# One more folding of the odd rows of a Fourier transform, and product tiles of more than 64 rows

## The chip, the cores and the metric

One core of one Trainium2 chip. The time is that of the device for one execution, in microseconds (us), on the slowest core; here there is only the one. A figure for a kernel is the median of its timed runs. PE is TensorE (PEld its weight loads, which put the stationary operand of a product in place), DVE is VectorE, ACT is ScalarE, POOL is GpSimd. PSUM and SBUF are the two memories of the core that the kernel works in: its products are written to PSUM, which it uses in parts called banks; most else lies in SBUF. A "product" below is one matmul of the source; in float32 it is two PE instructions.

## The reference, cut to what matters

```python
def _attn_ref(x):                       # x: 8 x 3008 x 256
    X = np.fft.fft(x, axis=1)
    X = np.fft.fft(X, axis=2)
    return X.real.astype(np.float32)

def _moe_ref(x, w_in, w_out):           # 24064 x 256, 256 x 2048, 2048 x 256
    h = x @ w_in
    r = np.maximum(h, 0.0)
    g = r * r
    return (g @ w_out).astype(np.float32)
```

Eight sequences of 3008 rows. The transform along the rows is a product with cosine and sine tables. Row n and row 3008 - n have equal cosines and opposite sines, so rows are added and subtracted ("folded") before the product, which halves its length; the same is done again for other symmetries of the table.

## The kernel before: the parts that matter here

Each sequence takes 48 steps: 6 blocks of 251 (or 250) columns by 8 chunks of the hidden layer. A step makes four products `ph` (into the hidden layer), evaluates relu squared, and does seven products `mA` to `mD` of the step two before (out of the hidden layer). While sequence b is in its steps, the transform of sequence b + 1 is done on the side, cut into small pieces that `between()` slips in after each half of a step, at a steady pace.

```python
def class_tiles(S):                    # rows of the folded transform, in classes
    half = S // 8 + 1
    tiles = []
    for c, order in enumerate((range(0, half, 4), range(2, half, 4), range(1, half, 2), range(half, S // 4 + 1))):
        for r in range(0, len(order), P):                       # P = 128
            tiles.append((c, order[r], order.step, len(order[r:r + P])))
    return tiles                       # 95 | 94 | 128, 60 | 128, 128, 120 rows

    def fold(b, t): ...                # DVE: makes wP, wQ of tile t of sequence b

    def dft_ops(b):
        def group(kp, which):          # kp: even or odd k; which: P (cosine) or Q (sine)
            def product(ps, c):
                for t in ts:           # the tiles of class c
                    nc.tensor.matmul(ps, w, tab[0:rows, kp, PLACE[t]:PLACE[t] + NC[kp][c]],
                                     start=t == ts[0], stop=t == ts[-1])
            def even_n():              # classes 0, 1, 2: 95, 94, 128 and 60 rows
                ...
            def odd_n():               # class 3: 128, 128 and 120 rows, 376 or 377 columns
                st["odd"] = psd.tile([P, 512], F32, name="pd", tag="d")[0:n, 0:n0]
                product(st["odd"], 3)
            # join_4, join_2, join_1: DVE adds and subtracts the parts
    ...
    def between():                     # called after each half of a step
        nonlocal spent
        if i < 2 * NJ:
            return
        spent -= pace
        while side and spent <= 0:
            t, f = side.pop(0)
            f()
            spent += t
```

"E" is one special column of the transform, done once for all later sequences while sequence 0 is in its steps.

## Time and profile before

| | before |
|---|---|
| median of 3 runs | 1990.51 us (1989.71 to 1991.41) |
| span of the profiled run | 1991.9 us |
| PE busy | 1957.8 us, 98% |
| DVE, ACT, POOL busy | 70%, 45%, 58% |
| one sequence in its steady state | 237.8 us, PE busy in all of it |

The first rows say that PE sets the time; the last, that it does so without a pause. A saving must therefore be PE time, and a new cost on another engine matters only where PE comes to wait for it. The lines themselves are in the prediction.

### The profile page before, as it was taken

Reading aid. Unit: us, or ns where it says so; the run is one execution under the profiler, and the core shown is the slowest. Engines: PE = TensorE matmul, PEld = TensorE weight load, DVE = VectorE, ACT = ScalarE, POOL = GpSimd, SP = SyncE. Lnnn points to the kernel's source line nnn. Section 1 sums busy time; section 2 is a strip of 40 time slices with the busy share of each in tenths; the row PEclk is TensorE's granted clock in tenths of the full one; section 3 lists DMA queues with packets and bytes.
Section 4 is the critical chain, followed back from the end, with each engine's and each line's share of the span. In section 5 each row is a group of like instructions: output and inputs, shape, how many; then the busy total and the mean of one; then the engine's idle time right before and its main releaser. Section 6 shows DMA issues by size and latency. Waiting matters only on the chain.

```text
span 1991.9 us, 27283 instructions
## 1 busy us (share of the span) xinstructions
PE 1957.8 (98%) x9104; PEld 1701.1 (85%) x9104; DVE 1391.3 (70%) x3492; ACT 896.2 (45%) x973; POOL 1158.8 (58%) x1695
## 2 busy tenths in 40 slices
PE   6999999999999999999999999999999999999998
PEld 3788888888888888888888888888888888888887
DVE  7889867776578765787558875677756876555554
ACT  1654444444444444444344443444444444445443
POOL 0037646666566655666557665666656675566664
PEclk8999999999999999999999999999999999999999
DMA  6331101110011111111011110121002100100100
GB/s 190 110 39 47 38 11 37 47 27 22 18 46 32 40 19 27 27 41 39 11 32 32 39 30 11 32 51 29 22 11 52 32 11 16 32 11 11 22 11 21
DMA packets 144687, 68.49 MB, mean 34 GB/s; under 512 B 128440, under 2 KB 135547, under 8 KB 144546
## 3 DMA queue, kind: packets, MB, share of 16 engines
q1 hardware_dynamic: 143470, 66.24, 14.1%
q8 instruction: 71, 1.16, 0.2%
q14 instruction: 70, 0.57, 0.1%
q10 hardware_dynamic: 1076, 0.52, 0.1%
HBM read 42.03 MB, written 24.68 MB: 33 GB/s over the span
## 4 chain that ended last, share of the span: by engine, by line
PE 94%; DVE 2%; DMA 1%; ACT 1%; SPq 0%; issue 0%; DVEq 0%; ACTq 0%
PE ph L412 16%; PE ph L413 16%; PE mA L465 16%; PE mC L465 16%; PE mB L465 16%; PE mD L465 8%; PE pd L349 5%; DMA xt<-in_x_dram 1%; DMA raw<-in_moe_w_in_dram 1%; DVE he L415 0%; DVE g L418 0%; ACT g L427 0%; ACT g L428 0%; SPq L163 0%; DVE g L417 0%
## 5 line engine op out<-in xcount | busy, mean ns | idle before, releaser
L427 ACT ACTIVATE g<-g 128x1004 f32<-128x1004 f32 (+1 forms) x384 | 399.6, 1041 | 894.3 <-DVE g L418 511.1
L415 DVE SCALAR_TENSOR_TENSOR he<-Et,gE,ph 128x251 f32<-128x251 f32 (+1 forms) x768 | 361.8, 471 | 476.6 <-PE ph L413 475.1
L435 POOL TENSOR_TENSOR s<-g 128x251 f32<-128x251 f32 (+1 forms) x376 | 248.9, 662 | 739.3 <-ACT g L428 668.1
L412 PE MATMUL ph<-Pt,G 128*128 128x251 f32 (+1 forms) x1536 | 453.4, 376 | 4.5 <-ACT G L237 3.4
L413 PE MATMUL ph<-Qt,G 127*128 127x251 f32 (+1 forms) x1536 | 451.3, 374 | 0.2 <-DVE Qt L362 0.2
L428 ACT ACTIVATE g<-g 128x1004 f32<-128x1004 f32 (+1 forms) x384 | 399.3, 1040 | 12.1
L465 PE MATMUL mC<-s,wsum 128*128 128x251 f32 (+1 forms) x1504 | 381.3, 374 | 0.0
L465 PE MATMUL mA<-g,wout 128*128 128x251 f32 (+1 forms) x1504 | 381.0, 375 | 0.0
L417 DVE TENSOR_TENSOR g<-he,ph 128x251 f32<-128x251 f32 (+1 forms) x768 | 320.6, 417 | 55.6 <-POOL s L437 0.5
L412 PEld LDWEIGHTS ph<-Pt,G 128*128 128x128 f32 x1536 | 287.2, 189 | 48.7 <-ACT G L237 4.0
L413 PEld LDWEIGHTS ph<-Qt,G 127*128 127x128 f32 x1536 | 291.1, 190 | 36.4 <-DVE Qt L362 0.6
L465 PEld LDWEIGHTS mA<-g,wout 128*128 128x128 f32 x1504 | 282.5, 189 | 41.7 <-issue 2.9
L465 PEld LDWEIGHTS mC<-s,wsum 128*128 128x128 f32 x1504 | 285.5, 190 | 34.5
L418 DVE TENSOR_TENSOR g<-he,ph 128x251 f32<-128x251 f32 (+1 forms) x768 | 314.2, 409 | 0.0
L436 POOL TENSOR_TENSOR s<-s,g 128x251 f32<-128x251 f32 (+1 forms) x376 | 282.0, 750 | 29.4
L437 POOL TENSOR_TENSOR s<-g 128x251 f32<-128x251 f32 (+1 forms) x376 | 291.4, 775 | 0.0
L438 POOL TENSOR_TENSOR s<-g,s 128x251 f32<-128x251 f32 (+1 forms) x376 | 246.0, 654 | 0.0
L465 PE MATMUL mB<-g,wsum 128*128 128x251 f32 (+1 forms) x752 | 220.5, 374 | 0.0
L465 PE MATMUL mD<-s,wout 128*128 128x251 f32 (+1 forms) x752 | 220.3, 374 | 0.0
L465 PE MATMUL mB<-s,wout 128*128 128x251 f32 (+1 forms) x752 | 219.9, 374 | 0.0
L465 PEld LDWEIGHTS mB<-g,wsum 128*128 128x128 f32 x752 | 142.6, 190 | 17.4
L465 PEld LDWEIGHTS mD<-s,wout 128*128 128x128 f32 x752 | 141.9, 189 | 17.7
(85 smaller groups left out, 1264.3 us busy)
## 6 DMA issues: line engine op xcount, KB each, us to landing
out_dram<-os SPq DMA_DIRECT2D x376, 56.0 KB
xt<-in_x_dram SPq DMA_DIRECT2D x24, 512.0 KB
xt<-in_x_dram SPq DMA_DIRECT2D x16, 384.0 KB
Et<-e_dram SPq DMA_DIRECT2D x7, 752.5 KB
out_dram<-os SPq DMA_DIRECT2D x288, 6.8 KB
raw<-in_moe_w_in_dram SPq DMA_DIRECT2D x16, 256.0 KB
raw<-in_moe_w_out_dram SPq DMA_DIRECT2D x16, 256.0 KB
xt<-in_x_dram SPq DMA_DIRECT2D x8, 480.0 KB
```

The lines of the kernel that those rows point to most:

```text
L412: nc.tensor.matmul(hP, G1[:, fs], pt[:, ks], start=True, stop=True)
L413: nc.tensor.matmul(hQ, G2[:, fs], qt[:, ks], start=True, stop=True)
L415: nc.vector.scalar_tensor_tensor(out=t, in0=et[:, ks], scalar=gE[:, fc:fc + 1], in1=hP, op0=ALU.mult, op1=ALU.add)
L417: tt(out=g[:, h, 0, 0:n], in0=t, in1=hQ, op=ALU.add)
L418: tt(out=g[:, h, 1, 0:n][:, ::-1], in0=t, in1=hQ, op=ALU.subtract)
L427: act(v, v, AF.Relu)
L428: act(v, v, AF.Square)
L435: gt(out=s1, in0=g21, in1=g22, op=ALU.add)
L436: gt(out=s2, in0=s1, in1=g11, op=ALU.subtract)
L437: gt(out=s3, in0=g11, in1=g21, op=ALU.subtract)
L438: gt(out=s4, in0=g12, in1=s2, op=ALU.subtract)
L465: nc.tensor.matmul(acc[nm][:, i, 0:n], w, v[:, 0:n], start=j == 0 and i == 0, stop=j == NJ - 1, skip_group_check=True)
```

## The change

The odd n of the later sequences are folded once more: row n is combined with the row mirrored within the odd set, and the cosine and sine parts of k even and odd part ways. The product is then over two tiles in place of three, for each half of the columns by itself. It needs, per sequence, a reversal of rows (a shuffle on DVE and loads in pieces of 32 rows), additions, and multiplications by a cosine and a sine per row. 188 mirrored rows are 128 + 60; the 60 are padded with zeros to 128. The tables of the odd class are sorted into even and odd columns once, after the pass for E, which still uses them unsorted. And the class of 188 rows is cut into 96 and 92, not 128 and 60. The side work of sequence 0 starts a block earlier, at half pace.

```diff
+        size = -(-len(order) // -(-len(order) // P) // R) * R          # 96
-        for r in range(0, len(order), P):
-            tiles.append((c, order[r], order.step, len(order[r:r + P])))
+        for r in range(0, len(order), size):
+            tiles.append((c, order[r], order.step, len(order[r:r + size])))
 ...
+        def f_turn():
+            w = w_of(t)
+            if i == 0:
+                st["v"], st["w"] = w_of(ODD0), w
+                nc.vector.stream_shuffle(w, w, REVERSE)
+            else:
+                st["v"], st["w"] = w, w_of(NT)
+                nc.vector.stream_shuffle(st["w"][0:H // 2], w[H // 2:P], REVERSE)
+                nc.gpsimd.memset(st["w"][H // 2:P], 0.0)
+            spare("f0", "f0")
+            nc.scalar.copy(st["f0"][rows], st["v"][rows, 0])
+        def spare(nm, tag):
+            st[nm] = fp.tile([P, D], F32, name=nm, tag=tag, bufs=1)
+            return st[nm]
+        def sine(to, src, signs):
+            for part, a in zip(PART, signs):
+                nc.scalar.mul(to[rows, part], src[rows, 1, part], turn[rows, 1 + a, i:i + 1])
+        def f_even():
+            v, w, a = st["v"][rows, 0], st["w"][rows, 0], st["f0"][rows]
+            tt(out=v, in0=a, in1=w, op=ALU.add)
+            tt(out=w, in0=a, in1=w, op=ALU.subtract)
+            sine(spare("f1", "f1"), st["w"], (0, 1))
+            sine(spare("f2", "f0"), st["v"], (1, 0))
+        def f_odd(): ...                                   # two scalar_tensor_tensor on DVE
 ...
             def odd_n():
+                for part in range(2):
+                    if kp:   ...  to = ps[:, part * nq:part * nq + nq]
+                    else:    ...  to = ps[:, part:n0:2]            # every second column of PSUM
+                    for i, pair in enumerate(((ODD0, ODD0 + 1), (ODD0 + 2, NT))):
+                        nc.tensor.matmul(to, folded[b, pair[other]][:, kp, PART[which]][:, 0:n],
+                                         columns(tab, ODD0 + i, o), start=i == 0, stop=i == 1)
 ...
-        if i < 2 * NJ:
+        if i < NJ:
             return
-        spent -= pace
+        spent -= pace / 2 if i < 2 * NJ else pace
```

(Cut: the loads, the sorting of the tables on ACT, the joins of the new parts for odd k, the weights of the pieces, and the order of the side work of sequence 0, in which the pass for E now comes before the groups of sequence 1.)

More of the change, by code (lines that the diff above doesn't have):

```diff
@@ L112 @@
     fp = ctx.enter_context(tc.tile_pool(name="fp", bufs=2))
-    wp = ctx.enter_context(tc.tile_pool(name="wp", bufs=NT))
+    wp = ctx.enter_context(tc.tile_pool(name="wp", bufs=NT + 1))
     pq = ctx.enter_context(tc.tile_pool(name="pq", bufs=2))
@@ L129 @@
     xt = {}
-    def load_x(b, t):
-        _, r0, step, rows = TILES[t]
+    ODD0 = NT - 3
+    HALF = S // 16
+    REST = HALF - P
+    ODD = [[(0, 0, P)],
+           [(p, 2 * HALF - p - R, R) for p in range(0, P, R)],
+           [(0, P, H // 2)] + [(H // 2 + p, 2 * HALF - P - p - R, R) for p in range(0, H // 2, R)]]
+    assert H == P and REST <= H // 2 and TILES[ODD0][0] == 3 and TILES[ODD0 + 1][1] == TILES[ODD0][1] + P
+    def load_x(b, t):
+        c, r0, step, rows = TILES[t]
+        if b and c == 3:
+            xt[b, t] = xp.tile([P, 4, D], F32, name="xt", tag="x")
+            for p, first, count in ODD[t - ODD0]:
+                nc.sync.dma_start(out=xt[b, t][p:p + count], in_=x[b, S // 8 + 1 + first:S // 8 + 1 + first + count])
+            return
         while rows % 15 and rows % 16 and r0 + step * rows < NROW:
@@ L263, with make_turn, part_table, columns @@
     PQE = {}
+    PART = (slice(0, H + 1), slice(H + 1, D))
+    REVERSE = list(range(R - 1, -1, -1))
+    turn = const.tile([P, 3, 2], F32, name="turn")
+    def make_turn():
+        for i in range(2):
+            for a, tab in enumerate((cosT, sinT, sinT)):
+                nc.scalar.mul(turn[:, a, i:i + 1], tab[:, 1, PLACE[ODD0 + i]:PLACE[ODD0 + i] + 1], -1.0 if a == 2 else 1.0)
+    rows_used = const.tile([P, 1], F32, name="rows_used")
+    nc.vector.memset(rows_used, 0.0)
+    nc.vector.memset(rows_used[0:REST], 1.0)
+    def part_table(tab, i):
+        nk, at = NC[0][3], PLACE[ODD0 + i]
+        v = tab[:, 0, at:at + nk]
+        a = op.tile([P, nk], F32, name="tp", tag="os")
+        nc.scalar.mul(a, v, rows_used if i else 1.0)
+        nc.scalar.copy(v[:, 0:(nk + 1) // 2], a[:, 0::2])
+        nc.scalar.copy(v[:, (nk + 1) // 2:], a[:, 1::2])
+    def columns(tab, t, part):
+        nk, at = NC[0][3], PLACE[t]
+        nq = (nk + 1) // 2
+        return tab[:, 0, at + part * nq:at + (nk if part else nq)]
     NE = B - 1
@@ L266 @@
     e_dram = dp.tile([NE, NKT], F32, name="e_dram")
-    e_rows = const.tile([NE, NKT], F32, name="e_rows")
     def load_column(t):
@@ L285, in fold @@
     def fold(b, t):
-        r = slice(0, TILES[t][3])
+        odd = b > 0 and t >= ODD0
+        r = slice(0, P if odd else TILES[t][3])
         st = {}
@@ L312, in f_dc, with w_of @@
             tt(out=new(fp, "dc", [P, 2, H - 1])[r], in0=d[r, :, 1:H], in1=d[r, :, D - 1:H:-1], op=ALU.subtract)
+        def w_of(t):
+            if (b, t) not in folded:
+                folded[b, t] = wp.tile([P, 2, D], F32, name="w", tag="w")
+            return folded[b, t]
         def f_p():
-            sc, wP = st["sc"], new(wp, "wP", [P, 2, H + 1])
+            sc, w = st["sc"], w_of(t)
             for kp in range(2):
-                tt(out=wP[r, kp], in0=sc[r, 0], in1=sc[r, 1], op=ALU.subtract if kp else ALU.add)
@@ L318, in f_p @@
-            folded[b, t, 0] = wP
+                tt(out=w[r, kp, PART[0]], in0=sc[r, 0], in1=sc[r, 1], op=ALU.subtract if kp else ALU.add)
         def f_q():
-            dc, wQ = st["dc"], new(wp, "wQ", [P, 2, H - 1])
+            dc, w = st["dc"], w_of(t)
             for kp in range(2):
-                tt(out=wQ[r, kp], in0=dc[r, 0], in1=dc[r, 1], op=ALU.add if kp else ALU.subtract)
-            folded[b, t, 1] = wQ
-        return [(0.7, f_s), (0.7, f_d), (0.5, f_sc), (0.4, f_dc), (0.6, f_p), (0.6, f_q)]
+                tt(out=w[r, kp, PART[1]], in0=dc[r, 0], in1=dc[r, 1], op=ALU.add if kp else ALU.subtract)
@@ new lines, in fold @@
+        ops = [(0.9, f_s), (0.9, f_d), (1.2, f_sc), (0.6, f_dc), (0.9, f_p), (0.7, f_q)]
+        if not odd or t == ODD0:
+            return ops
+        i = t - ODD0 - 1
+        rows = slice(0, TILES[ODD0 + i][3] if i == 0 else REST)
+        def f_turn():
[9 more added lines that the diff above has]
+            nc.scalar.copy(st["f0"][rows], st["v"][rows, 0])
@@ L328, in dft_ops, with f_odd @@
+        def f_odd():
+            for nm, u in (("f1", "v"), ("f2", "w")):
+                u = st[u][rows, 1]
+                nc.vector.scalar_tensor_tensor(out=u, in0=u, scalar=turn[rows, 0, i:i + 1], in1=st[nm][rows],
+                                               op0=ALU.mult, op1=ALU.add)
+        return ops + [(0.8, f_turn), (1.2, f_even), (1.4, f_odd)]
     def dft_ops(b):
@@ L345, in product @@
                     rows = TILES[t][3]
-                    w = we[t] if b is None else folded[b, t, which % 2]
-                    w = w[0:rows, kp]
+                    w = (we[t] if b is None else folded[b, t][:, :, PART[which % 2]])[0:rows, kp]
                     w = w[:, H:H + 1].to_broadcast([rows, n]) if which == 2 and b is not None else w[:, 0:n]
@@ L378, in odd_n, with join_odd @@
             def odd_n():
-                st["odd"] = psd.tile([P, 512], F32, name="pd", tag="d")[0:n, 0:n0]
-                product(st["odd"], 3)
+                ps = psd.tile([P, 512], F32, name="pd", tag="d")[0:n]
+                st["odd"] = ps[:, 0:n0]
+                if not b:
+                    return product(ps[:, 0:n0], 3)
+                nq = (n0 + 2) // 2 if kp else (n0 + 1) // 2
+                for part in range(2):
+                    if kp:
+                        tab, o = (cosT, sinT)[part], 0
+                        to = ps[:, part * nq:part * nq + nq]
+                        other = part != which
+                    else:
+                        tab, o = (cosT, sinT)[which], part
+                        to = ps[:, part:n0:2]
+                        other = part != which
+                    for i, pair in enumerate(((ODD0, ODD0 + 1), (ODD0 + 2, NT))):
+                        nc.tensor.matmul(to, folded[b, pair[other]][:, kp, PART[which]][:, 0:n],
+                                         columns(tab, ODD0 + i, o), start=i == 0, stop=i == 1)
+                if kp:
+                    st["cos"] = hp.tile([P, nq], F32, name="oc", tag="oc", bufs=1)[0:n]
+                    nc.scalar.copy(st["cos"], ps[:, 0:nq])
+                    st["sin"] = ps[:, nq:2 * nq]
+            def join_odd():
+                a, ps = st["cos"], st["sin"]
+                nq = a.shape[-1]
+                st["odd"] = o = hp.tile([P, NC[1][3]], F32, name="do", tag="do", bufs=1)[0:n, 0:n0]
+                tt(out=o[:, 0::2], in0=a[:, 0:nq - 1], in1=ps[:, 0:nq - 1], op=ALU.add)
+                if which == 1:
+                    tt(out=o[:, 1::2], in0=ps[:, 1:nq], in1=a[:, 1:nq], op=ALU.subtract)
+                else:
+                    tt(out=o[:, 1::2], in0=a[:, 1:nq], in1=ps[:, 1:nq], op=ALU.subtract)
             def join_1():
-                dst = e_rows if b is None else PQE[b][which]
+                dst = PQE[1][2][0:n] if b is None else PQE[b][which]
                 nh = S // 8
@@ L386, in join_1 @@
                      st["odd"])
-            return [(0.5, even_n), (0.5, join_4), (0.7, join_2), (0.0, odd_n), (1.2, join_1)]
+            ops = [(0.1, even_n), (0.5, join_4), (0.7, join_2), (0.1, odd_n), (1.0, join_1)]
+            if b and kp:
+                ops.insert(4, (0.7, join_odd))
+            return ops
         ops = [] if b is None else [(0.0, start)]
@@ L394, in dft_ops @@
         if b is None:
-            ops.append((0.0, lambda: nc.sync.dma_start(out=e_dram[:, :], in_=e_rows)))
+            ops.append((0.0, lambda: nc.sync.dma_start(out=e_dram[:, :], in_=PQE[1][2][0:NE])))
         return ops
@@ L533, in ahead @@
     def ahead(b):
-        ops = [piece for t in range(NT) for piece in fold(b, t)] + dft_ops(b)
-        if b == 1:
-            ops += [(0.6, lambda t=t: fold_column(t)) for t in range(NT)] + dft_ops(None)
-        return ops + [(0.0, lambda: load_e(b))] if b else ops
+        folds = [piece for t in range(NT) for piece in fold(b, t)]
+        if b > 1:
+            return folds + dft_ops(b) + [(0.0, lambda: load_e(b))]
+        start, *groups = dft_ops(1)
+        tables = [(0.3, lambda tab=tab, i=i: part_table(tab, i)) for i in range(2) for tab in (cosT, sinT)]
+        return (folds + [start] + [(0.6, lambda t=t: fold_column(t)) for t in range(NT)] + dft_ops(None) + tables
+                + groups + [(0.0, lambda: load_e(1))])
     weights = [lambda j=j: load_win(j) for j in range(2)]
@@ L630 @@
                 load_column(i - NJ)
+            if i == NJ:
+                make_turn()
             if i % per == 0:
@@ L633 @@
                 side = ahead(b + 1) if b + 1 < B else []
-                spent, pace = 0.0, sum(t for t, _ in side) / (2 * (per - (0 if i else 2 * NJ)) - 6)
+                spent, pace = 0.0, sum(t for t, _ in side) / (2 * per - 6 - (0 if i else 3 * NJ))
             g = front(b, k0, n, j, between)
```

## The prediction

> **What bounds the kernel now.** I read the page's busy shares first, then equal windows over the run, then the chain of work that ended last inside one period, then the weight loads around one small product.
>
> ```profile
> PE 1957.8 (98%) x9104; PEld 1701.1 (85%) x9104; DVE 1391.3 (70%) x3492; ACT 896.2 (45%) x973; POOL 1158.8 (58%) x1695
> ```
>
> ```profile
> 467.20:704.90 237.70, 237.70 (x1114) 208.23 (x1113) 167.24 (x418) 107.27 (x113) 148.90 (x216) 1.00 0.13 30
> 704.90:942.70 237.80, 237.80 (x1115) 208.35 (x1114) 167.42 (x418) 107.36 (x113) 148.88 (x216) 1.00 0.13 30
> ```
>
> The window columns are the stretch, its length, then busy us (and instructions) of PE, PEld, DVE, ACT and POOL, clock, DMA share, GB/s. One sequence takes 237.8 us (the same spot in the chain recurs at 467.16, 704.93, 942.70), and PE is busy in all of it at full clock: no wait, no transfer and no other engine sets the time there. The others have room (DVE 167.4 of 237.8, ACT 107.4, POOL 148.9). So what PE no longer does in a period comes off the end, as long as the others still keep up. The chain of waits within a period says what a sequence's transform costs PE:
>
> ```profile
> 963.50 0.42 PE ph L413 x2
> 963.92 1.28 PE pd L349 x8
> 965.20 0.62 PE ph L412 x2
> 965.83 0.42 PE ph L413 x2
> ...
> 974.33 0.43 PE ph L413 x2
> 974.75 1.90 PE pd L349 x6
> 976.65 0.42 PE ph L412 x2
> ```
>
> Columns: start, us on the chain, what. Each product in the source is two PE instructions. The eight are the even-n half of a group (tiles of 95, 94, 128 and 60 rows), the six its odd-n half (three tiles of 376 or 377 columns). Two things to see: the six take 1.90 us, 317 ns each for 376 columns; and the pair after the eight takes 0.62 us where every other such pair takes 0.42, so an even half really costs 1.28 + 0.20 = 1.48 us. The weight loads show why:
>
> ```profile
> 963.76 0.64 PEld L349 LDWEIGHTS pd<-cosT,wP 95*128 95x128 f32 x5
> 964.62 0.29 PEld L349 LDWEIGHTS pd<-cosT,wP 60*128 60x128 f32 x2 [0.22 <-issue]
> 965.13 0.19 PEld L412 LDWEIGHTS ph<-Pt,G 128*128 128x128 f32 x1 [0.22 <-issue]
> ```
>
> The same in the waits summed over the run (us, times, longest us):
>
> ```profile
> PEld pd L349 <- issue: 17.3, 64, 1.1
> ```
>
> The loads of 95, 94 and 128 rows run on without a gap. Before the 60-row loads and again before the 128-row load behind them there are 0.22 us in which nothing waited for data; the last line says that such a wait happens 64 times. Model check: 48 steps of 22 instructions at 0.2124 us (0.85 us per four) = 224.3 us, plus 4 groups of 1.48 + 1.90 us = 13.5, gives 237.8. The period is explained to 0.1 us.
>
> **What the Trainium skill says.** (1) "TensorEngine Tiling (Array Packing)", Key Properties: "Mode switching requires drain", with a 64-row mode for contractions of 64 rows or fewer. The trace agrees: only the 60-row tile has the gaps, twice 0.22 us. (2) "TensorE: Matmul & The Clock Gate", LDWEIGHTS (loading the stationary operand): time goes with the columns, columns/1.2 ns, so 107 ns for 128, whatever the rows. The trace's five loads in 0.64 us with the last lasting 0.19 are (0.64-0.19)/4 = 0.11 us apart: agrees, and makes 94 or 95 columns load-bound. (3) "PSUM — Partial Sum Buffer", Specifications (TRN2): 8-byte cachelines, non-contiguous patterns slow matmuls significantly. The change writes every second PSUM column, so this matters. The kernel before has such a write only in its last transposes:
>
> ```profile
> 1982.68 0.48 PE L514 MATMUL po<-ident,c 128*125 128x128 f32 x2 [0.50 <-DVE c L492]
> ```
>
> One of them shows as 0.37 us and two as 0.48, so they start 0.11 us apart for 128 columns, no slower than a product's half (251 columns in 0.212 us). It speaks against a penalty, but transposes don't accumulate, so not conclusively. (4) "VectorE: DVE Perf Modes", the perf-mode tier table: STREAM_SHUFFLE about 2400 ns for 2048 elements; for 512 I estimate 0.65 us. No run so far shows it.
>
> **The change, part by part.**
> (a) Odd n folded once more, sequences 1 to 7 (4 groups each, 28 in all). Three products of 376 or 377 columns become four of 188 or 189. An instruction costs 2 cycles per column: 317 ns for 376 columns is 314 + 3; 189 columns make 157.5 + 3.3 = 161 ns, above the 110 ns of a load. Eight make 1.29 us instead of 1.90: 0.61 us a group, 28 x 0.61 = 17.2 us, all on PE.
> (b) Tiles of 96 and 92 rows for 128 and 60. The work in columns stays, the mode switches go. An even half is then four starts of 0.110 (95 columns, load-bound) and four of 0.161: 1.08 us against 1.48, or 0.40 a group; 28 x 0.40 = 11.2 us. So a period falls by 4 x 1.01 = 4.1 us, to 233.7.
> (c) The same tiles in the E pass (two groups) and in sequence 0: about 0.3 us for each E group, 0.6. At the start most even groups lie before data that is waited for; only the two of Q between 44.0 and 47.8 us are on the chain: 0.9 us.
> (d) Added to DVE per sequence: two shuffles (1.3 us), four additions of 256 (4 x 0.42, the duration at 251), four scalar-tensor operations (4 x 0.47), four joins of 188 columns (4 x 0.345): 6.3 us. 167 becomes about 173 of 233.7: beside PE. To ACT: two copies of 256 (0.36 each), eight scalings of about 128 (estimated 0.3 each from copies of 95 at 0.236 and 256 at 0.376), two copies of 189 (0.32): 3.8 us. POOL gets one memset. None is on the path in a steady period; the shuffle, the copy, the additions and the last operations are separate pieces, each at least half a step (2.3 us) apart in most places.
> (e) Once, in sequence 0: ACT sorts four tables (each a scaling of 377 columns, about 0.5 us, and two copies of 0.32), 4.6 us bunched in about one step beside 2.1 us of activations. The odd products wait for them. Consumption of g lags two steps (9.3 us), so I allow at most 2 us.
> (f) The side work of sequence 0 starts at step 8 instead of 16, at half pace first. There DVE already has four weight subtractions a step (1.16 us). Its room:
>
> ```profile
> 100.00:120.00 20.00, 19.02 (x94) 16.72 (x94) 16.34 (x37) 13.54 (x22) 0.00 (x0) 1.00 0.27 67
> 120.00:140.00 20.00, 20.00 (x95) 17.77 (x94) 16.53 (x45) 9.56 (x11) 10.58 (x16) 1.00 0.36 16
> ...
> 200.00:220.00 20.00, 18.97 (x87) 15.96 (x86) 19.42 (x46) 7.85 (x8) 13.62 (x20) 1.00 0.19 48
> ```
>
> 16.5 of 20 us, and about 1 us a step (4 us in 20) is added: full, with a loss of perhaps 1 us. Later, at 200 to 220 us, where DVE at 19.4 now costs PE 1.0 us, the folds are spread thinner: up to 1 us gained. The first tile of x is asked for at 104 us and used near 117, so no new wait.
> Sum: 17.2 + 11.2 + 0.6 + 0.9 = 29.9, less about 1.4 for (e) and (f): 28.5. 1990.5 - 28.5 = 1962.
>
> **The rivals.** First, striding in PSUM: for even k (14 groups) the two parts interleave. If that doubled the time of those products, 14 x 1.29 = 18 us come back: 1980. The skill's sentence speaks for it, the transposes against; 15%. Second, DVE becomes the bound: the added 6.3 us and the chain PE, ACT copy, join delay the next evacuation, and PE waits for its two ph buffers. For it: 19.4 of 20 us in one window costs PE already. Against: a third of DVE is idle in all later periods, and an odd half already made DVE wait for PE without PE losing anything. If each of 28 groups lost 0.4 us, 11 us come back: 1973; 10%. Third, the gaps at 60 rows might not be from the row count but from the switch of table or output; then (b) gains nothing: 1973. The 120-row and 95-row loads have no gap, so 5%. Fourth, sequence 0 chokes on DVE or on the tables: 5 to 8 us, 1968; 10%.
>
> **Range and chances.** The arithmetic of (a) and (b) rests on measured spacings, so without a rival I expect 1958 to 1966. With the rivals' tail: 1957 to 1975. A gain of over 2% needs 39.8 us, 10 more than PE's whole saving: 4%. A loss of over 2% would need a stall in every period larger than all that is saved: 1%.
>
> **What would show it.** Period 233.7 us with PE busy throughout; the even half eight instructions in 1.08 us with the next pair at 0.42 and no gap in the weight loads; the odd half 1.29 us for even k and odd k alike; waits "pd <- issue" nearly gone; DVE near 173 us a period; in the first 320 us PE idle as before within 2 us. Wrong if the even-k odd half takes over 1.6 us, if PE shows idle time in later periods behind DVE or ACT, or if sequence 0 grows.

## More of the kernel before

At the end of a block, the accumulated `mA` to `mD` are read out. They have one PSUM bank each, and the first product of the next block overwrites `mA`:

```python
    def gather(n, plain, final):
        ...
        nc.scalar.copy(sA[:, :, 0:n], mA[:, :, 0:n])
        if not final:
            nc.scalar.copy(sB[:, :, 0:n], mB[:, :, 0:n])
```

## The result, and the profile after

| | before | after |
|---|---|---|
| median | 1990.82 us (5 runs) | 1968.72 us (1967.67 to 1969.33, 5 runs) |
| ratio | | 0.9885 (95%: 0.9872 to 0.9899) |
| one steady sequence | 237.8 us | 234.6 us |
| DVE busy in it | 167.4 us | 177.4 us |
| ACT busy in it | 107.4 us | 111.1 us |

Ratios, here and below, are those of the record, which takes them from the fast runs of both kernels; they are not quite the ratios of the quoted medians. The gain is 22.1 us by the medians; the prediction's point was 28.5. The length of a sequence is the time from the first `ph` product of one to that of the next in the trace.

The page's first line, and windows of two sequences (columns as in the prediction's windows):

```profile
PE 1925.7 (98%) x9160; PEld 1705.0 (87%) x9160; DVE 1459.2 (74%) x3606; ACT 927.8 (47%) x1075; POOL 1168.2 (59%) x1702
```

```profile
724.62:959.21 234.59, 234.06 (x1122) 209.08 (x1121) 177.35 (x434) 111.15 (x124) 150.82 (x218) 1.00 0.11 31
959.21:1193.80 234.59, 234.05 (x1122) 209.08 (x1121) 177.26 (x434) 111.06 (x124) 150.79 (x218) 1.00 0.12 31
```

PE is busy 234.06 of 234.59 us: for the first time there is a pause, about half a microsecond by this count. Now the chain of waits in one sequence (start, us on the chain, what), around an even half (eight instructions of L440) and two odd halves (eight of L485; the first for even k, the second for odd k):

```profile
953.02 0.42 PE ph L537 x2
953.45 1.09 PE pd L440 x8
954.54 0.85 PE mA L589 x4
...
959.21 1.28 PE pd L485 x8
960.49 0.85 PE mA L589 x4
...
970.93 1.28 PE pd L485 x8
972.21 0.85 PE mA L589 x4
```

The even half takes 1.09 us where it took 1.28 plus 0.20 behind it; the four `mA` instructions behind it take their usual 0.85. The odd half takes 1.28 us instead of 1.90, for even k with its strided PSUM columns exactly as for odd k without. In the weight loads of such an even half nothing is left of the gaps:

```profile
953.08 1.17 PEld L440 LDWEIGHTS pd<-cosT,w 95*128 95x128 f32 x8
954.22 0.77 PEld L589 LDWEIGHTS mA<-g,wout 128*128 128x128 f32 x4
```

So both savings came as worked out: 4 x (0.39 + 0.62) = 4.0 us a sequence. But the sequence became only 237.77 - 234.58 = 3.2 us shorter. The timeline at the one place where PE pauses, once a sequence (start, us, engine, line, operation; the bracket is the idle time before and what ended it):

```profile
943.14 1.01 PE L589 MATMUL mA<-g,wout 128*128 128x251 f32 x4
...
944.64 0.69 ACT L403 ACTIVATE f<-w,turn 60x129 f32<-60x129 f32 x2 [0.36 <-DVE w L392]
...
945.81 0.63 DVE L407 TENSOR_TENSOR w<-f,w 60x256 f32<-60x256 f32 x1
...
946.47 0.73 DVE L408 TENSOR_TENSOR w<-f,w 60x256 f32<-60x256 f32 x1
...
947.30 0.69 ACT L403 ACTIVATE f<-w,turn 60x129 f32<-60x129 f32 x2 [1.97 <-DVE w L408]
...
947.90 0.56 ACT L605 COPY sA<-mA 128x502 f32<-128x502 f32 x1
...
948.51 1.11 PE L589 MATMUL mA<-g,wout 128*128 128x251 f32 x4 [0.53 <-ACT sA L605]
```

Read it from the bottom. The first product of a new block (948.51) waits for the copy of `mA`. The last products into `mA` had ended by 944.2, so for `mA`'s part the copy could have run three microseconds earlier. But ACT works in order, and ahead of the copy stand the two pairs of scalings of `f_even`. The first pair ran at 944.64. The second then left ACT idle for 1.97 us, until DVE had finished the second addition (L408). Why should it wait for that? It reads the odd-k half of `v`, which the additions do not touch. The diff tells: `spare("f2", "f0")` takes the buffer of `f0`, and `f0` is what both additions read. It is a wait for a buffer, not for data. The start of one PE instruction to the start of the next is 0.90 us there and 0.21 us at other products of 251 columns: 0.70 us lost in each of sequences 1 to 5, and 0.97 in sequence 6 (sequence 7 has no side work).

### The profile page after: what moved, and what is told of

It reads as the page before. It is cut to its first block, busy times and chain, and to the rows that moved or that the text cites. A ratio compares the mean times of both kernels' runs of the same rounds, so it can differ in the third digit from the quotient of the medians.

```text
span 1965.9 us, 27667 instructions
## 1 busy us (share of the span) xinstructions
PE 1925.7 (98%) x9160; PEld 1705.0 (87%) x9160; DVE 1459.2 (74%) x3606; ACT 927.8 (47%) x1075; POOL 1168.2 (59%) x1702
## 4 chain that ended last, share of the span: by engine, by line
PE 91%; DVE 4%; ACT 2%; DMA 1%; issue 1%; SPq 0%; POOL 0%; DVEq 0%; ACTq 0%; POOLq 0%
PE mA L589 16%; PE mC L589 16%; PE ph L537 16%; PE ph L536 16%; PE mB L589 16%; PE mD L589 8%; PE pd L440 2%; PE pd L485 2%; DVE he L539 1%; DMA xt<-in_x_dram 1%; DVE g L542 1%; DVE g L541 1%; DMA raw<-in_moe_w_in_dram 1%; ACT g L551 0%; ACT g L552 0%
## 5 line engine op out<-in xcount | busy, mean ns | idle before, releaser
L559 POOL TENSOR_TENSOR s<-g 128x251 f32<-128x251 f32 (+1 forms) x376 | 241.8, 643 | 713.7 <-ACT g L552 672.4
L542 DVE TENSOR_TENSOR g<-he,ph 128x251 f32<-128x251 f32 (+1 forms) x768 | 314.2, 409 | 0.0
L560 POOL TENSOR_TENSOR s<-s,g 128x251 f32<-128x251 f32 (+1 forms) x376 | 289.7, 771 | 29.4
L561 POOL TENSOR_TENSOR s<-g 128x251 f32<-128x251 f32 (+1 forms) x376 | 292.6, 778 | 0.0
L562 POOL TENSOR_TENSOR s<-g,s 128x251 f32<-128x251 f32 (+1 forms) x376 | 253.9, 675 | 0.0
L589 PEld LDWEIGHTS mB<-g,wsum 128*128 128x128 f32 x752 | 142.6, 190 | 17.4
```

What stands on the lines that cost most here:

```text
L542: tt(out=g[:, h, 1, 0:n][:, ::-1], in0=t, in1=hQ, op=ALU.subtract)
L559: gt(out=s1, in0=g21, in1=g22, op=ALU.add)
L560: gt(out=s2, in0=s1, in1=g11, op=ALU.subtract)
L561: gt(out=s3, in0=g11, in1=g21, op=ALU.subtract)
L562: gt(out=s4, in0=g12, in1=s2, op=ALU.subtract)
L589: nc.tensor.matmul(acc[nm][:, i, 0:n], w, v[:, 0:n], start=j == 0 and i == 0, stop=j == NJ - 1, skip_group_check=True)
```

## The experiments

Three theories of those 0.70 us. **A:** the reused buffer, as just read. **B:** DVE has become too full, and whatever waits for it runs late. **C:** the scalings take up ACT ahead of the copy, waiting or not. Four kernels ran on one chip in the same rounds.

**The changed kernel again (control).** No edit.

> Control: the changed kernel once more, beside the others on one chip. In its profile every sequence from 1 to 5 lasts 234.59 us, of which about 0.70 us is one PE gap at the first mA product of the second block, behind the ACT copy of mA (sA). Expected again: 1968 to 1970 us, the same gap, sequence length 234.6 us.

Measured: 1968.30 us (1966.98 to 1968.77), ratio 0.9882 (0.9867 to 0.9897); sequences of 234.58 us with the same gap. The result repeats.

**A buffer of its own.** The second pair of scalings goes into the buffer of a join, which is idle while folding goes on:

```diff
-            sine(spare("f2", "f0"), st["v"], (1, 0))
+            st["f2"] = hp.tile([P, NC[1][3]], F32, name="f2", tag="do", bufs=1)[:, 0:D]
+            sine(st["f2"], st["v"], (1, 0))
```

> The second pair of scalings in the folding of the 60-row part is written into another buffer, one that lies idle then, in place of the one that the two additions read. Theory A (reused buffer): ACT works in order, its second pair of scalings waits until the additions have read the buffer, the copy of mA stands behind it, and mA has one PSUM bank, so PE waits; then the gap of 0.70 us goes, a sequence lasts 233.9 us and the run is 4 to 5 us shorter than the control. Theory B (VectorE is simply too full): no change, 234.6 us. Theory C (the four scalings take up ACT ahead of the copy, whatever they wait for): about half the gap stays, 234.2 us or more.

Measured: 1963.51 us (1961.63 to 1964.81), ratio 0.9858 (0.9843 to 0.9873): 4.8 us under the control's median. Sequences of 233.78 us. The same place in ACT's timeline:

```profile
944.33 1.28 ACT L403 ACTIVATE f<-w,turn 60x129 f32<-60x129 f32 x4 [0.37 <-DVE w L392]
945.51 0.56 ACT L606 COPY sA<-mA 128x502 f32<-128x502 f32 x1
```

All four scalings now run in one go, before the additions, and the copy follows at once, although the same ACT work stands ahead of it. And the windows of two sequences:

```profile
720.36:954.14 233.78, 233.78 (x1122) 209.14 (x1121) 177.23 (x435) 110.89 (x125) 149.74 (x218) 1.00 0.11 31
954.14:1187.92 233.78, 233.78 (x1122) 209.15 (x1121) 177.67 (x435) 110.95 (x125) 150.06 (x218) 1.00 0.11 31
```

PE is busy in all of it again, with DVE and ACT as busy as before the edit (177.4 and 110.9 us). That speaks for A, against B (DVE has as much to do) and against C (ACT has as much to do). This version is also faster than both kernels: the 95% intervals of its ratio and of the control's overlap a little (up to 0.9873, from 0.9867), but no run of one reaches the range of the other (at most 1964.81 against at least 1966.98), and the traces show 0.80 us less in each of five sequences.

**Scalings later.** The additions and the scalings become two pieces, the buffers stay shared:

```diff
             tt(out=w, in0=a, in1=w, op=ALU.subtract)
+        def f_sine():
             sine(spare("f1", "f1"), st["w"], (0, 1))
             sine(spare("f2", "f0"), st["v"], (1, 0))
 ...
-        return ops + [(0.8, f_turn), (1.2, f_even), (1.4, f_odd)]
+        return ops + [(0.8, f_turn), (0.6, f_even), (0.6, f_sine), (1.4, f_odd)]
```

> The scalings are a piece of side work of their own, issued a step part after the additions, the buffers as in the change. Theory A: by then the additions are done, ACT does not wait, and unless the new place falls on another copy of mA the gap goes: 233.9 us a sequence, 4 to 5 us shorter than the control. Theory B: no change. Theory C: the same ACT work, so a gap stays if it still lies ahead of the copy.

Measured: 1964.92 us (1964.05 to 1966.14), ratio 0.9866 (0.9852 to 0.9881); sequences of 233.78 us, no gap. The shared buffer does no harm once ACT is handed the scalings after the additions are done. That fits A and speaks against B. It does not tell A from C: in sequence 2 of the trace the copy of `mA` starts at 712.33 us and the scalings at 716.14, so their new place lies behind the copy.

**Scalings on DVE.**

```diff
-                nc.scalar.mul(to[rows, part], src[rows, 1, part], turn[rows, 1 + a, i:i + 1])
+                nc.vector.tensor_scalar(out=to[rows, part], in0=src[rows, 1, part],
+                                        scalar1=turn[rows, 1 + a, i:i + 1], scalar2=None, op0=ALU.mult)
```

> The scalings go from ACT to VectorE (eight more instructions of about 0.2 us a sequence). Theory A: ACT has nothing to wait for there, the gap goes although VectorE does about 1.6 us more a sequence: 233.9 us, 4 to 5 us shorter than the control. Theory B: VectorE is fuller, so the gap grows or new ones come: over 234.6 us. Theory C: the gap goes too, as in A.

Measured: 1964.63 us (1962.76 to 1966.15), ratio 0.9867 (0.9851 to 0.9883); sequences of 233.78 to 234.13 us, the `mA` gap gone. More DVE work and yet a shorter time: B falls as the cause of the gap. But the sequences are no longer all at 233.78: in sequences 1 to 6 of the trace PE starts late six times, 0.7 us in all, and the one late start that the trace puts down to an engine (0.21 us at 1183.64) waited for DVE. So DVE seems not far from its limit in the stretch where folding is done.

**The wait made longer, with and without the shared buffer.** The first addition is done three times (the result is the same), once in the changed kernel and once in the kernel with a buffer of its own:

```diff
-            tt(out=v, in0=a, in1=w, op=ALU.add)
+            for _ in range(3):
+                tt(out=v, in0=a, in1=w, op=ALU.add)
```

> The changed kernel with the first of the two additions done three times (same result), so that the buffer it reads is held two additions longer (0.42 to 0.63 us each as the trace has them). Theory A (the wait for that buffer stands ahead of the copy of mA): the gap of 0.70 us a sequence grows by what the two additions take, to 1.5 to 2.0 us, and a sequence lasts 235.4 to 235.9 us, 5 to 9 us more in all than the changed kernel's 1968. Theory B (VectorE too full): growth too.

Measured: 1972.61 us (1972.04 to 1974.28), ratio 0.9907 (0.9892 to 0.9922); sequences of 235.51 us. The timeline at the same place:

```profile
950.22 0.69 ACT L403 ACTIVATE f<-w,turn 60x129 f32<-60x129 f32 x2 [2.90 <-DVE w L409]
950.81 0.55 ACT L606 COPY sA<-mA 128x502 f32<-128x502 f32 x1
...
951.42 1.11 PE L590 MATMUL mA<-g,wout 128*128 128x251 f32 x4 [1.47 <-ACT sA L606]
```

ACT's idle time ahead of the second scalings went from 1.97 to 2.90 us, PE's gap from 0.70 to 1.63 us, and the sequence grew by 0.93: the three are one quantity.

> The same additions three times in the kernel with a buffer of its own for the second scalings. Theory A: ACT never waits for the additions, so the same added VectorE work costs nothing: 233.8 us a sequence, about 1963.5 us. Theory B: it costs as much as in the run with the shared buffer.

Measured: 1968.09 us (1965.05 to 1968.65), ratio 0.9880 (0.9865 to 0.9894); sequences of 234.16 to 234.67 us. The gap at `mA` is absent, as A has it. But "costs nothing" was wrong: four more additions a sequence brought PE late starts of about 0.2 us behind DVE, some 0.6 us a sequence in place of 0.93. By the medians the added work cost 4.6 us here (over 1963.51) and 4.3 us with the shared buffer (over the control's 1968.30), against other rounds: the totals of this pair don't tell A from B. What does is the place of the loss, 1.63 us at `mA` in one kernel and none there in the other. So A names the 0.70 us of the change, by this and above all by the buffer of its own, and B is the limit just behind it.

**The two parts of the change by themselves.** Only the tile sizes, in the kernel before:

```diff
-        for r in range(0, len(order), P):
-            tiles.append((c, order[r], order.step, len(order[r:r + P])))
+        size = -(-len(order) // -(-len(order) // P) // R) * R
+        for r in range(0, len(order), size):
+            tiles.append((c, order[r], order.step, len(order[r:r + size])))
```

> The kernel before with nothing but the odd-residue tiles of 96 and 92 rows in place of 128 and 60. Prediction's part (b): an even half falls from 1.48 to 1.08 us, a sequence from 237.77 to 236.2 us, 11.2 us in sequences 1 to 7, with the E pass and the start 12 to 14 us in all: about 1978 us against 1991. Rival (the gaps come from changing table or output, not from the row count): the gaps stay, 1991 us.

Measured: 1980.65 us (1979.27 to 1982.99), ratio 0.9949 (0.9934 to 0.9963); sequences of 236.21 to 236.24 us, as expected. The total is 10.2 us under the median of before, where 12 to 14 were expected: the E pass gave less than its 0.6 (see below), and the start gave nothing clear. Only the second folding, by `size = P` in the changed kernel:

> The changed kernel with the tiles of 128 and 60 rows put back: the second folding alone. Part (a): the odd halves keep 1.28 us, the even halves go back to 1.48 us, the PE gap of 0.7 us behind ACT may stay or move. A sequence of about 236.1 us with the gap, 235.3 without; 1980 to 1983 us. If the two parts were not additive (an engine other than PE setting the time) only_tiles and old_tiles would together save clearly more or less than the 22 to 23 us of the change.

Measured: 1979.16 us (1978.74 to 1983.86), ratio 0.9945 (0.9931 to 0.9960); sequences of 236.12 to 236.42 us, with the gap at `mA` in each (0.7 us in four of them, 0.97 in two). By the medians of the same rounds (before 1990.85) the parts give 10.2 and 11.7 us, together 21.9; the change gave 22.1. They add up, as parts of one engine's time do.

**Where the mode switches begin.** The kernel before with 124 and 64 rows, and with 123 and 65 (`size = 124 if c == 2 else P`, and 123):

> The kernel before with 124 and 64 rows for 128 and 60. If the switch of mode happens at 64 rows or fewer[...], the 64-row products have the same two gaps of 0.22 us: as the kernel before, 1990 to 1992 us, a sequence of 237.8 us.

Measured: 1991.71 us (1990.92 to 1993.27), ratio 1.0002 (0.9985 to 1.0018); sequences of 237.76 to 237.78 us.

> The kernel before with 123 and 65 rows: one row over 64. By the same theory no gap is left: a sequence of 236.2 us and about 1978 us, the same as only_tiles. If the cost grew smoothly with a tile being small, this would lie next to rows_124_64.

Measured: 1980.33 us (1978.11 to 1981.60), ratio 0.9945 (0.9930 to 0.9959); sequences of 236.21 to 236.24 us. One row in a tile decides: the even half is 1.28 us on the chain, and 0.2 us more behind it, for 64 rows, and 1.09 with nothing behind it for 65. That the gaps are a drain at a switch of mode is a reading, which the prediction takes from the skill; the runs show the gaps and the row count, not what PE does in them. The waits of the weight loads, summed over the run, first with 64 and then with 65 rows:

```profile
PEld pd L350 <- issue: 18.8, 69, 1.1
```

```profile
PEld pd L350 <- issue: 5.7, 18, 1.1
```

Behind 325 us, where sequence 1 begins, the run with 64 rows has 24 of these waits (5.3 us), one for each even half of sequences 1 to 6; the run with 65 has none.

**The early start of sequence 0's side work taken back,** in the kernel with a buffer of its own:

```diff
-        if i < NJ:
+        if i < 2 * NJ:
             return
-        spent -= pace / 2 if i < 2 * NJ else pace
+        spent -= pace
 ...
-                spent, pace = 0.0, sum(t for t, _ in side) / (2 * per - 6 - (0 if i else 3 * NJ))
+                spent, pace = 0.0, sum(t for t, _ in side) / (2 * (per - (0 if i else 2 * NJ)) - 6)
```

> The kernel with the buffer of its own, and the side work of sequence 0 begun at step 16 again as before the change, at a pace to match, in place of step 8 at half pace. Prediction's part (f) had the early start cost about 1 us and give back up to 1 us. If the early start was needed (VectorE too full later in sequence 0), sequence 0 grows from 265.4 us by 2 to 6 us; if it was not, it stays within 1 us.

Measured: 1967.45 us (1967.06 to 1969.88), ratio 0.9883 (0.9867 to 0.9900). Sequence 0 takes 270.67 us in the trace where it took 265.37; the others 233.78 as before. Between 165 and 251 us PE starts seven times too late at a `ph` product, 5.2 us in all; the waits in that stretch (us, times, longest us; very short ones left out) name DVE:

```profile
PE ph L537 <- DVE g L543: 4.0, 5, 1.2
```

The early start is worth 4 us by the medians (of different rounds), 5.3 by the traces.

## Why the prediction was right

The time lay in the range (1957 to 1975), and a change within 2% was the likeliest forecast. Point by point, by its steps:

- **Part (a), the odd halves:** 1.29 us predicted, 1.28 measured, for even and odd k. Right. (The split of 317 ns into 314 + 3 comes out of two measured lengths: 212.4 ns for 251 columns and 317 for 376 lie on about 0.83 ns a column and 3 to 4 ns besides.)
- **Part (b), the even halves:** 1.08 us predicted, 1.09 measured, and 236.2 us a sequence when done alone. Right; the experiment with 64 and 65 rows shows that the row count is the cause, so the third rival (the gaps come from something else) fell. But not all of the 64 waits "pd <- issue" were of this kind, as the prediction read them: 24 lay in the later sequences, one for each even half, and are gone; 19 remain, all in the first 320 us, so "nearly gone" holds only for the later sequences.
- **The period:** 233.7 us predicted (4 x 1.01 is 4.04 and not 4.1, which hardly matters), 234.6 measured; 233.78 with the one buffer separated. "PE shows idle time in later periods behind DVE or ACT" was one of the prediction's own signs of being wrong, and it came. The failed step is in (d): "None is on the path in a steady period". I had set the pieces' durations and distances against each other and found room, but not asked what the scalings wait for and what stands behind them in ACT's queue. `f_even` issues additions on DVE and scalings on ACT in one piece, so the distance of half a step between pieces does not lie between those two, and the shared buffer ties them. By the lengths of the sequences with and without the shared buffer it cost 0.80 us in five of them and 1.07 in the sixth, 5.1 us in all (the gap itself and a slower restart behind it); the medians say 4.8. That is most of the 6.4 us by which the point was off: with the buffer separated the medians of its rounds give 27.7 us, where 28.5 were predicted. That the small terms come out so near is partly luck, since the 1.4 us taken off for (e) and (f) was not lost, and the E part of (c) gave 0.2 us for 0.6. The second rival had this shape (PE waits behind ACT and DVE) but named another wait, the two `ph` buffers, and a size of 11 us.
- **DVE:** 173 us a sequence predicted, 177.4 measured. The new operations came to 8.3 to 8.6 us a sequence and not 6.3. The term that was mis-sized is the duration: I took 0.42 us for an addition of 256 columns and 0.47 for the other kind from operations that read PSUM. The new ones read SBUF twice, and lasted longer on average (a shuffle took 0.73 to 0.74 us, estimated at 0.65):

```profile
L542 DVE TENSOR_TENSOR g<-he,ph 128x251 f32<-128x251 f32 x640 | 261.9, 409 | 0.0
L415 DVE SCALAR_TENSOR_TENSOR w<-w,turn,f 128x256 f32<-128x256 f32 x14 | 9.6, 727 | 0.0
...
L408 DVE TENSOR_TENSOR w<-f,w 128x256 f32<-128x256 f32 x7 | 5.7, 810 | 0.2
```

  (Columns of these groups of the changed kernel: count, busy us and mean ns, idle before.) The rest of the rise was in the folds that were there before: their last two pieces, additions that read SBUF twice, took 13.9 us a sequence before and 17.0 to 17.4 after. The prediction had no term for that. The Trainium skill, "SBUF — State Buffer", Who interferes with whom, says that a DVE instruction with two SBUF inputs contends with a GpSimd instruction that reads SBUF, and one with at most one SBUF input outside the two-port modes does not. The trace agrees: of the DVE additions of 129 columns with both inputs in SBUF (L370), the 19 that no GpSimd instruction overlapped took 283 to 296 ns, the 74 that one overlapped throughout took 322 to 814 ns, 564 on average; of the new L415, of all sizes, the 3 without overlap took 470 to 478 ns, as I had assumed, and the 10 overlapped throughout took 931 to 947; L542, which reads PSUM, took 407 to 419 ns either way. No run took POOL's work away, so this is read from the trace and not tested.
- **ACT:** 3.8 us more a sequence predicted, 3.7 measured.
- **(c), E and the start:** 0.3 us predicted for each E group. Its even half went from 1.16 to 1.07 us, and the 0.2 us behind it stayed, so 0.1 came. The stationary operand of E has 7 columns where the products around it have 127 or 128, and by the starts of its instructions PE loses 0.09 us ahead of each E half and 0.19 behind it, behind the odd half too, whose tiles have 128 and 120 rows: changing the rows can't remove that. No run changed those 7 columns. For the start 0.9 us was predicted. The first step begins at 54.49 us in the trace of before and between 50.55 and 54.94 in those of later kernels with the same start: no run settles it. It hides one more of the prediction's signs: in the first 320 us PE was to be idle as before within 2 us, and was idle 28.4 us in the trace of after against 25.7, the difference lying ahead of the first step.
- **(e), the tables sorted on ACT:** up to 2 us allowed, and between 260 and 269 us, where ACT sorts them in two lots (from 260.3 and from 267.1 us), PE has no gap but the 0.2 us behind a product of E. It cost nothing that shows.
- **(f), the early start:** expected to cost about 1 us and give back as much. Sequence 0 went from 270.62 to 266.07 us in the two traces, near what (a) and (b) give; without the early start it would have been 5 us longer. That the fourth rival did not come is owed to it.
- **The first rival, striding in PSUM:** did not come; 1.28 us with and without.

The profiled runs of before and after differ by 26.0 us and the medians by 22.1. By the traces the 26.0 are 2.6 us ahead of the first step, 4.6 in sequence 0, 18.8 in sequences 1 to 6 and 0.1 behind them. The first of these varies from run to run, as (c) shows, and the profiled run of before was 3 us above its median; why the start varies is not known. I compared medians for totals and traces for single sequences.

## What to carry to other kernels

Where PE was full, a model of starts (columns against weight load) gave the saving of a sequence to a tenth of a microsecond; the risk lies in what the new side work holds up. For every instruction added to an in-order engine, ask what it waits for, a reused buffer included, and what stands behind it that the bounding engine needs. And take durations from an instruction with the same memories as operands, not only the same shape, and with the same work going on beside it.

## What the Trainium skill lacked or had wrong

- "PSUM — Partial Sum Buffer", Specifications (TRN2), has any non-contiguous pattern slow matmuls significantly. Here float32 products that write every second PSUM column took 1.28 us for eight instructions (754 columns), products into contiguous columns 1.28 us too (756 columns).
- "TensorEngine Tiling (Array Packing)", Key Properties, says that a switch of mode drains TensorE, but not that a plain product with a contraction of 60 or 64 rows among longer ones meets gaps, without any tile being asked for, nor what a switch costs: here two gaps of 0.22 us in the weight loads, 0.39 us on the path for one 64-row tile among longer ones (1.48 against 1.09 us), nothing at 65 rows. Nor does it say this of few columns: products whose stationary operand has 7 columns, among ones of 127 and 128, had 0.09 us ahead of them and 0.19 us behind.
